# Attention and two feed-forward layers on one core: range checks after the attention, weights put together by shifts, a bias table per head, v in two float16 parts, a first pass of six 512-wide chunks

## The chip, the cores and the metric

The kernel runs on one core of a Trainium2 chip. The metric is the device time of one execution in microseconds (us); for the kernel before it is 632.22 us, the median of three runs (631.07 to 633.04). A core has five engines with a queue each: TensorE (PE in the profile; its weight loads are PEld), VectorE (DVE), ScalarE (ACT), GpSimd (POOL) and SyncE (SP, which issues the DMAs). Each works through its own instructions in the order of the program and waits on semaphores for the others.

## The reference

Attention over 2 x 8 heads of 768 rows of 64, in which a row sees the first `n_global` keys and its last `n_local` ones, with a bias per head; then two feed-forward layers over 1536 rows of 512.

```python
scores = scale * np.matmul(q, k.transpose(0, 1, 3, 2))
keep = is_global | is_local                       # 8 first keys, or 0 <= row - key < 96
dist = np.where(is_global & ~is_local, float(n_local), np.abs(rel))
bias = -slopes[:, None, None] * dist[None, :, :]  # slopes: 2 ** -(h + 1) for 8 heads
a = softmax(np.where(keep, scores + bias, -1e9))
x = np.matmul(a, v) as 1536 x 512
h = x @ w_in                                      # 512 x 2048
x = (h * np.clip(h + 3.0, 0.0, 6.0) / 6.0) @ w_out
h = np.maximum(x @ w_in2, 0.0)
return (h * h) @ w_out2
```

The feed-forward weights arrive as float64, that is as two 32-bit words a number.

## The kernel before, in words

**Attention.** The 1536 rows are 12 tiles of 128. For each tile PE transposes q and k (T, L413), multiplies them head pair by head pair (L479 in float32 for the first six tiles, which the code calls plain; L488 in split float32r for the last six), DVE adds the bias and finds the row's extreme in one instruction (L502), ACT takes the exponential and its sum (L515), the weights are transposed (by PE in the plain tiles, L554; by a DMA in the others, after a split into two float16 parts, L324 and L535), PE multiplies them by v (L603), DVE divides by the sum (L624 to L627), PE transposes the result (x_T, L647), and ACT and DVE write it as two float16 parts (x_hi, L324; x_lo, L656). Those parts, kept for all rows in three blocks of 512 columns (`xt`), are what the feed-forward layers read. In the last six tiles v is three bfloat16 parts (L324, L450), and the product takes five matmuls for each head and key block. q is first divided by the head's slope (L296), so that one bias table serves all heads.

**Weights.** A layer's 2048 inner columns are 16 chunks of 128; a chunk has two halves (of w_in and w_out), each a 128 x 512 tile of float64 pairs. For each of the 64 halves DVE masks the exponent (L777), ACT shifts it to float32's place (L781), DVE puts the sign to it (L784), takes the mantissa's upper bits (L790) and adds the lower word (L791), POOL multiplies the two (L796), and the result is written as two float16 parts (L324 or L326, then L804). A chunk takes one of 23 slots; 12 of these are there during the attention, the others take the attention's space when it has ended.

**Feed-forward.** An item is one chunk with one block of rows: 12 matmuls up (L848), a gate on ACT and DVE (L861 to L873), a split into two float16 parts (L324 or L326, L881), and 12 matmuls down (L914 in the first layer, L917 in the second), three for each product since both sides are in two parts. The first layer goes in three passes: in the first, 5 chunks with blocks of 256 rows, so that work for PE begins when two tiles of the attention are done; then 6 and 5 chunks with blocks of 512. The sums of a pass are added to `acc` in SBUF. The second layer is one pass of 16 chunks. In PSUM the attention holds 4 of 8 banks, the sums of the first pass 2 (`r_c`), the products up 2.

**Range checks.** Every split of a weight, and every tile of x, is squared and summed by ACT into a column of `gd` (L342); with the gates' sums these are compared at the end, and decide whether a slower version of the whole is to run afterwards.

**Order.** A planner (`Plan.order`) knows for each operation the engines that can do it, a duration, its buffers and a priority, and from these lays out once, when the program is built, what every engine does in which order; shifts of the priorities stand in a table (`SHIFT`). Where PE would wait early on, it puts in filler matmuls on a blank tile (L293).

Of the kernel before, what the change touches and what calls it, by code (L numbers as in the profile page):

```python
# [18 lines left out]
P = 128  # L19

N1 = 5
SLOTS_A = 12
SLOTS = 23
# [153 lines left out]
class Kern:  # L177
# [26 lines left out]
    def setup(self, pool):  # L204
# [48 lines left out]
        self.ebias_s = pool.tile([P, 1], F32, name="ebias_s")  # L253
        nc.gpsimd.memset(self.ebias_s, -(896.0 + 20.0 - EW) * 2.0 ** 23)
# [23 lines left out]
        self.scale_q("DVE", self.raw_t[0][0])  # L278
# [24 lines left out]
    def band_pools(self, ctx):  # L303
# [8 lines left out]
        self.kt = const.tile([P, 2, NP, 3, P], F32R, name="kt")  # L312
        pool = lambda name, bufs: ctx.enter_context(tc.tile_pool(name=name, bufs=bufs))
# [21 lines left out]
    def check_op(self, plan, view, deps, use, prio, n=512):  # L335
# [19 lines left out]
    def attention_ops(self, plan):  # L355
# [10 lines left out]
        for t in range(NT):  # L366
# [58 lines left out]
            for i, (c, t_, a_, b_, place) in enumerate(ends):  # L425
# [9 lines left out]
                if not plain:  # L435
                    qe.append(op(c + "_lo", {"DVE": 0.6}, lo, deps=[h_], use=[a_, b_], prio=vt - 4.3 + i / 10))
# [382 lines left out]
    def ffn_ops(self, plan, items, x_done):  # L819
# [9 lines left out]
        for it in items:  # L829
# [91 lines left out]
            for a in range(nacc):  # L921
# [7 lines left out]
                if acq:  # L929
                    state["g2"] = u  # L930
# [239 lines left out]
```

## Time and profile before

| | |
|---|---|
| median of three runs | 632.22 us |
| the profiled execution | 631.7 us |
| its span, first to last instruction | 629.9 us |
| PE busy | 599.6 us, 95% |
| DVE busy | 460.6 us, 73% |
| ACT busy | 331.8 us, 53% |
| POOL busy | 151.4 us, 24% |
| matmuls in the profile | 3887 |

Times in the views are microseconds from the span's start. The ends of matmuls are modelled, so what one costs in a dense stretch is read from the distance between two starts. A duration of DVE or ACT reaches a little into that of the next instruction.

### The profile page before, as it was taken

Reading aid. Unit: us, or ns where it says so; the run is one execution under the profiler, and the core shown is the slowest. Engines: PE = TensorE matmul, PEld = TensorE weight load, DVE = VectorE, ACT = ScalarE, POOL = GpSimd, SP = SyncE. Lnnn points to the kernel's source line nnn. Section 1 sums busy time; section 2 is a strip of 40 time slices with the busy share of each in tenths; the row PEclk is TensorE's granted clock in tenths of the full one; section 3 lists DMA queues with packets and bytes.
Section 4 is the critical chain, followed back from the end, with each engine's and each line's share of the span. In section 5 each row is a group of like instructions: output and inputs, shape, how many; then the busy total and the mean of one; then the engine's idle time right before and its main releaser. Section 6 shows DMA issues by size and latency. Waiting matters only on the chain.

```text
span 629.9 us, 10465 instructions
## 1 busy us (share of the span) xinstructions
PE 599.6 (95%) x3887; PEld 345.6 (55%) x3887; DVE 460.6 (73%) x1036; ACT 331.8 (53%) x778; POOL 151.4 (24%) x155
## 2 busy tenths in 40 slices
PE   7998798988989999999999999999999999999994
PEld 6887797777876544444444443444444444444442
DVE  4999989997889899999989999994333333333331
ACT  4997689888966665455586767552121111211111
POOL 1324427344442242314222431230000000000000
PEclk9999899999999999999999999999999999999998
DMA  9753648877652342324133232320010000100002
GB/s 181 192 139 107 181 107 187 149 133 109 124 126 93 101 134 100 101 67 135 67 101 101 67 132 69 101 67 1 1 67 1 0 1 0 68 1 0 1 0 72
DMA packets 84699, 53.32 MB, mean 85 GB/s; under 512 B 62368, under 2 KB 78752, under 8 KB 84640
## 3 DMA queue, kind: packets, MB, share of 16 engines
q1 hardware_dynamic: 84640, 52.57, 32.1%
q8 instruction: 32, 0.52, 0.3%
q14 instruction: 27, 0.22, 0.1%
HBM read 42.99 MB, written 3.15 MB: 73 GB/s over the span
## 4 chain that ended last, share of the span: by engine, by line
PE 46%; DVE 33%; DMA 10%; ACT 6%; issue 3%; POOL 0%; SPq 0%; DVEq 0%; ACTq 0%
PE bank L848 19%; PE bank L917 15%; DVE y L791 6%; DVE gt L881 5%; DMA wr<-in_moe_w_in_dram 4%; DVE e L784 4%; DMA pt<-ph 4%; DVE y L790 4%; PE bank L603 3%; PE bank L914 3%; DVE g L871 2%; DVE e L777 2%; DVE w L804 1%; DMA vp<-vp 1%; PE bank L479 1%
## 5 line engine op out<-in xcount | busy, mean ns | idle before, releaser
L848 PE MATMUL bank<-xt,w 128*128 128x512 f16 (+1 forms) x936 | 208.0, 338 | 1.1 <-DVE g L871 1.0
L796 POOL TENSOR_TENSOR y<-y,e 128x512 f32<-128x512 f32 x64 | 87.2, 1362 | 197.8 <-DVE y L791 91.5
L848 PEld LDWEIGHTS <-w 128*128 128x128 f16 x936 | 90.4, 98 | 72.1 <-issue 1.8
L914 PE MATMUL bank<-gt,w 128*128 128x256 f16 (+1 forms) x612 | 120.5, 317 | 0.9 <-DVE gt L881 0.8
L873 DVE SCALAR_TENSOR_TENSOR g<-bank,g 128x512 f32<-128x512 f32 x48 | 33.1, 690 | 117.3 <-ACT g L863 117.3
L863 ACT ACTIVATE g<-bank 128x512 f32<-128x512 f32 x48 | 28.5, 593 | 158.2 <-PE bank L848 158.0
L848 PE MATMUL bank<-xt,v 128*128 128x512 f16 x396 | 107.0, 379 | 0.0
L917 PEld LDWEIGHTS <-gt 128*128 128x128 f16 x576 | 56.3, 98 | 71.7 <-DVE gt L881 3.8
L917 PE MATMUL bank<-w,gt 128*128 128x512 f16 x324 | 86.8, 379 | 0.2 <-DVE gt L881 0.2
L881 DVE TENSOR_TENSOR gt<-g,gt 128x512 f16<-128x512 f32 (+1 forms) x99 | 73.9, 748 | 8.3 <-ACT gt L324 6.7
L914 PEld LDWEIGHTS <-w 128*128 128x128 f16 x612 | 59.4, 98 | 36.7 <-issue 1.7
L917 PE MATMUL bank<-v,gt 128*128 128x512 f16 x252 | 68.6, 379 | 1.2 <-DVE gt L881 1.2
L848 PEld LDWEIGHTS <-v 128*128 128x128 f16 x396 | 38.7, 98 | 46.3
L881 POOL TENSOR_TENSOR gt<-g,gt 128x256 f16<-128x256 f32 (+1 forms) x12 | 11.5, 959 | 201.8 <-DVE gt L326 192.7
L324 ACT ACTIVATE gt<-g 128x512 f16<-128x512 f32 (+1 forms) x64 | 34.5, 539 | 46.3 <-DVE g L871 37.1
L781 ACT ACTIVATE e<-e,ebias_s 128x512 int32<-128x512 int32 x64 | 45.7, 717 | 21.7 <-DVE e L777 21.3
L791 DVE SCALAR_TENSOR_TENSOR y<-wr,y 128x512 f32<-128x512 uint32 x64 | 51.8, 810 | 2.2
L784 DVE SCALAR_TENSOR_TENSOR e<-wr,e 128x512 int32<-128x512 int32 x64 | 47.5, 759 | 0.4 <-ACT e L781 0.4
L515 ACT ACTIVATE s<-s,mx 128x256 f32<-128x256 f32 (+1 forms) x96 | 46.0, 484 | 1.6 <-DVE mx L502 1.3
L861 ACT ACTIVATE g<-bank,half_s 128x512 f32<-128x512 f32 (+1 forms) x63 | 36.3, 577 | 19.7 <-PE bank L848 19.5
L914 PE MATMUL bank<-gt,v 128*128 128x512 f16 x144 | 38.9, 379 | 0.0
L871 DVE SCALAR_TENSOR_TENSOR g<-g,bank 128x512 f32<-128x512 f32 (+1 forms) x63 | 34.7, 552 | 4.9 <-ACT g L861 4.9
(118 smaller groups left out, 741.8 us busy)
## 6 DMA issues: line engine op xcount, KB each, us to landing
wr<-in_moe_w_in_dram SPq DMA_DIRECT2D x32, 512.0 KB, 4.0
wr<-in_moe_w_out_dram SPq DMA_DIRECT2D x32, 512.0 KB, 3.3
out_dram<-acc SPq DMA_DIRECT2D x12, 256.0 KB, 2.0
r<-in_q_dram SPq DMA_DIRECT2D x10, 256.0 KB, 3.4
r<-in_k_dram SPq DMA_DIRECT2D x10, 256.0 KB, 4.0
r<-in_v_dram SPq DMA_DIRECT2D x10, 256.0 KB, 3.6
acc<-in_q_dram SPq DMA_DIRECT2D x2, 256.0 KB, 4.6
acc<-in_k_dram SPq DMA_DIRECT2D x2, 256.0 KB, 5.1
```

The lines of the kernel that those rows point to most:

```text
L324: self.nc.scalar.activation(out=out, in_=in_, func=ACTF.Copy, scale=scale)
L515: nc.scalar.activation(out=s[:, e2, :n], in_=s[:, e2, :n], func=ACTF.Exp, scale=-1.0, bias=m["mx"][:, e2:e2 + 1], accum_out=sums[t][:, h:h ...
L781: nc.scalar.activation(out=d["e"], in_=d["e"], func=ACTF.Relu, scale=8.0, bias=self.eb)
L784: nc.vector.scalar_tensor_tensor(out=d["e"], in0=d["r"][:, :, 1], scalar=-2 ** 31, in1=d["e"], op0=ALU.bitwise_and, op1=ALU.bitwise_or)
L791: nc.vector.scalar_tensor_tensor(out=y.bitcast(F32), in0=d["r"].bitcast(U32)[:, :, 0], scalar=2.0 ** -32, in1=y, op0=ALU.mult, op1=ALU.add)
L796: self.tt(e)(out=y, in0=y, in1=d["e"].bitcast(F32), op=ALU.mult)
L848: nc.tensor.matmul(d["ps"], w[:, wi, 0, fs], xx[:, kd, o:o + n], start=(kd == 0 and i == 0), stop=(kd == self.KD - 1 and i == 2))
L861: nc.scalar.activation(out=g, in_=d["ps"], func=ACTF.Relu, scale=2.0 ** (EGD - EXW) / 6.0, bias=self.hf)
L871: nc.vector.scalar_tensor_tensor(out=g, in0=g, scalar=2.0 ** EGD, in1=ps, op0=ALU.min, op1=ALU.mult, **acc)
L881: self.tt(e)(out=gt[:, 1, :n], in0=d["g"], in1=self.val(gt[:, 0, :n]), op=ALU.subtract)
L914: nc.tensor.matmul(ps, w[:, wi, 1, s], g[:, gi, :n], start=st, stop=sp)
L917: nc.tensor.matmul(ps, g[:, gi, s], w[:, wi, 1, :], start=st, stop=sp)
```

## The change

- A bias table for each head (`first_h`, `band_h`, bfloat16) is made by 16 instructions on POOL at the start; q is no longer divided by the slope.
- A weight is put together from its two words by shifts: both words give a float32 pattern (two instructions on DVE), the sign and the upper exponent bits another (one), POOL multiplies them as before. ACT no longer takes part; it squares the second pattern as a range check instead.
- The checks on x and on the weights' split wait until the last tile of the attention is done; six more read v, which is loaded again for them.
- v is two float16 parts, and the product with v takes three matmuls in place of five.
- ACT makes the sum ready for the division (L620), in place of DVE.
- The first pass has 6 chunks with blocks of 512 rows. The splits of all six items of a block are kept (8 buffers in place of 3), and the products down go in two sweeps: first those of the output's columns 0 to 255, then those of 256 to 511, since two banks of PSUM hold only two of the four sums. 8 slots for chunks are there during the attention, 22 in all.
- The planner's durations, shifts and due times are other numbers.

```diff
-N1 = 5
-SLOTS_A = 12
-SLOTS = 23
+N1 = 6
+SLOTS_A = 8
+GB = N1 + 2
+SLOTS = 22
...
-    "v_0": 4.7, "v_1": 9.1, "v_2": -3.2, "v_3": -1.2, "v_glob": -5.2, "w_lo": 4.7, "w_load": -1.2, "w_man": 10.6,
+    "v_2": -3.2, "v_3": -1.2, "v_glob": -2.7, "v_load": -0.1, "w_exp": -23.4, "w_hi": 17.3, "w_lo": 1.3,
...
-    def scale_q(self, e, q):
-        self.tt(e)(out=q, in0=q, in1=self.qscale.unsqueeze(2).to_broadcast([P, self.H, self.D]), op=ALU.mult)
...
+        for to, src in ((self.first_h, self.first), (self.band_h, self.band.rearrange("p a c -> p (a c)"))):
+            for h in range(H):
+                nc.gpsimd.tensor_scalar(to[:, h], src, self.slope[h] * float(D) ** 0.5, 1.0, op0=ALU.mult, op1=ALU.mult)
...
-        self.sums2.append(plan.op("chk", {"ACT": 0.72}, emit, deps=deps, use=use, prio=prio))
+        self.sums2.append(plan.op("chk", {"ACT": 0.82}, emit, deps=deps + self.late, use=use, prio=prio))
...
-                vp_t[t] = self.vp_p.tile([P, 3, H * D], BF16, tag="vp", name="vp")
+                vp_t[t] = self.vp_p.tile([P, 2, H * D], F16, tag="vp", name="vp")
...
+                nc.vector.scalar_tensor_tensor(out=vp_t[t][:, 1], in0=raw[2].rearrange("p h d -> p (h d)"), scalar=2.0 ** EX,
+                                               in1=vp_t[t][:, 0], op0=ALU.mult, op1=ALU.subtract)
...
-                            out=s[:, e2, :n], in0=m["q"]["ps"][e2][:, p % 2, :n], in1=bias, scale=-self.slope[2 * p + e2],
+                            out=s[:, e2, :n], in0=m["q"]["ps"][e2][:, p % 2, :n], in1=bias, scale=-1.0 / float(D) ** 0.5,
...
-                                for l, parts in ((0, 3), (1, 2)):
+                                for l, parts in ((0, 2), (1, 1)):
...
-                nc.vector.tensor_scalar(rs, sums[t], 1e-9, 2.0 ** -EX, op0=ALU.add, op1=ALU.mult)
+                    nc.scalar.activation(out=rs, in_=sums[t], func=ACTF.Copy, scale=sx, bias=1e-9 * sx)
...
+                    nc.vector.tensor_scalar(y, d["r"][:, :, 1], 3, 0x7FFFFFFF, op0=ALU.logical_shift_left, op1=ALU.bitwise_and)
...
+                    nc.vector.scalar_tensor_tensor(out=y, in0=d["r"][:, :, 0], scalar=29, in1=y,
+                                                   op0=ALU.logical_shift_right, op1=ALU.bitwise_or)
...
+                    nc.vector.tensor_scalar(s, d["r"][:, :, 1], -2 ** 28, 0x30000000 ^ ((EW - 1) << 23), op0=ALU.bitwise_and,
+                                            op1=ALU.bitwise_xor)
...
+                    nc.scalar.activation(out=junk, in_=d["e"].bitcast(F32), func=ACTF.Square, scale=2.0 ** (128 - EW),
+                                         accum_out=self.gd3[:, i:i + 1])
...
-        r_h, r_c, r_g, r_t = self.r_h, self.r_c, Ring(3), Ring(2)
+        r_h, r_g, r_t = self.r_h, Ring(GB if self.fast else 3), Ring(2)
...
+            self.down_ops(plan, it, (0, 1) if half else (0, 1, 2, 3), vt + PELAG, state, acc_ops, x2_ops)
+            if half:
+                block.append(it)
+                if it["last"]:
+                    for k, i2 in enumerate(block):
+                        self.down_ops(plan, i2, (2, 3), vt + PELAG + 1 + 0.2 * k, state, acc_ops, x2_ops)
...
-            passes = [[(N1, 256), ((17 - N1) // 2, 512), ((16 - N1) // 2, 512)], [(16, 512)]]
+            passes = [[(N1, 512), ((17 - N1) // 2, 512), ((16 - N1) // 2, 512)], [(16, 512)]]
```

On PE, before, ahead of the fourth tile's x_T (L647), feed-forward matmuls (L848, L914) already stand between those of the attention:

```order
L848 LDWEIGHTS w_172
L848 MATMUL bank<-xt_0_165,w_172 128x256
L914 LDWEIGHTS w_171
L914 MATMUL bank<-gt,w_171 128x256
L479 MATMUL bank<-k_plain,q_plain 128x128 x8
L554 MATMUL bank<-ident,s 128x128 x4
L647 MATMUL bank<-ident,x 128x128 x4
```

The same place now, with x_T on L653, the product with v on L595 and the filler on L290:

```order
L595 MATMUL bank<-r_412,pt 128x64
L546 MATMUL bank<-ident,s 128x128 x8
L595 MATMUL bank<-r_933,pt 128x64
L653 MATMUL bank<-ident,x 128x128 x4
L479 MATMUL bank<-kt,qz_199 128x128 x4
L546 MATMUL bank<-ident,s 128x128 x4
L290 LDWEIGHTS blank
L290 MATMUL bank<-blank 128x256
```

Up to the fourth x_T there is now no feed-forward matmul, while 68 of the 79 fillers stand there; the first one comes after the fourth tile's x parts.

On POOL, behind the branch into the kernel, the tables now stand first, ahead of the copies of the global keys (L568; L576 before). Before:

```order
L576 COPY kg_plain<-k_plain 128x64 x2
L576 COPY k_plain<-kg_plain 128x2x32 x2
L796 TENSOR_TENSOR y<-y,e 128x512
L576 COPY k_plain<-kg_plain 128x2x32
L296 TENSOR_TENSOR r_511<-r_511,qscale 128x512
```

Now:

```order
L312 TENSOR_SCALAR first_h<-first 128x128 x8
L312 TENSOR_SCALAR band_h<-band 128x384 x8
L568 COPY kg_plain<-k_plain 128x64 x2
L568 COPY k_plain<-kg_plain 128x2x32 x4
L802 TENSOR_TENSOR y<-y,e 128x512 x2
```

The division of q (L296) is gone, and 16 instructions have come in front of the first copies.

## Rows read from the trace of the kernel before

**Rows 1.** The page's first part: busy time, share and instructions of each engine.

```profile
PE 599.6 (95%) x3887; PEld 345.6 (55%) x3887; DVE 460.6 (73%) x1036; ACT 331.8 (53%) x778; POOL 151.4 (24%) x155
```

**Rows 2.** Windows by stage: from:to length, busy (count) per engine, clock, DMA, GB/s.

```profile
6.00:183.00 177.00, 159.56 (x1791) 140.32 (x1792) 157.64 (x458) 148.59 (x423) 71.37 (x73) 0.98 0.69 148
...
200.00:340.00 140.00, 139.87 (x661) 64.45 (x660) 131.66 (x237) 85.51 (x168) 43.11 (x33) 1.00 0.31 102
...
430.00:622.00 192.00, 191.55 (x889) 86.73 (x887) 68.44 (x151) 27.81 (x47) 1.16 (x1) 1.00 0.03 12
```

**Rows 3.** Timeline of PE, 6 to 21 us: start, length, engine, line, shape, count.

```profile
7.09 0.63 PE L413 MATMUL bank<-ident,acc 128*128 128x128 f32 x4 [1.83 <-DVE acc L296]
...
16.96 0.56 PE L603 MATMUL bank<-acc,pt 128*128 128x64 f32 x4
17.36 0.49 PE L293 MATMUL bank<-blank 128*128 128x256 bf16 x3
17.78 1.16 PE L479 MATMUL bank<-k_plain,q_plain 64*128 64x128 f32 x16
18.87 1.09 PE L554 MATMUL bank<-ident,s 128*128 128x128 f32 x8
19.80 0.60 PE L647 MATMUL bank<-ident,x 128*128 128x128 f32 x4
```

**Rows 4.** Timeline of PE, 114 to 117.5 us.

```profile
114.84 0.76 PE L603 MATMUL bank<-vp,pt 128*128 128x64 bf16 x20 [0.78 <-DMA pt<-ph]
115.53 0.98 PE L488 MATMUL bank<-kt,qz 64*128 64x256 f32 x12
116.44 0.76 PE L603 MATMUL bank<-vp,pt 128*128 128x64 bf16 x20
```

**Rows 5.** Timeline of PE, 178 to 184 us: the last tile's x_T.

```profile
179.26 0.49 PE L848 MATMUL bank<-xt,w 128*128 128x256 f16 x3
179.59 0.49 PE L914 MATMUL bank<-gt,w 128*128 128x256 f16 x3
...
181.55 0.60 PE L647 MATMUL bank<-ident,x 128*128 128x128 f32 x4
```

**Rows 6.** Timeline of PE, 55 to 57.5 us: the fourth tile's x_T.

```profile
55.49 0.60 PE L647 MATMUL bank<-ident,x 128*128 128x128 f32 x4
```

**Rows 7.** Groups by line: busy us, mean ns of one, idle before them.

```profile
L791 DVE SCALAR_TENSOR_TENSOR y<-wr,y 128x512 f32<-128x512 uint32 x64 | 51.8, 810 | 2.2
L784 DVE SCALAR_TENSOR_TENSOR e<-wr,e 128x512 int32<-128x512 int32 x64 | 47.5, 759 | 0.4 <-ACT e L781 0.4
L781 ACT ACTIVATE e<-e,ebias_s 128x512 int32<-128x512 int32 x64 | 45.7, 717 | 21.7 <-DVE e L777 21.3 <-DVE k_plain L576 0.2
L790 DVE TENSOR_SCALAR y<-wr 128x512 int32<-128x512 int32 x64 | 36.7, 573 | 0.0
L777 DVE TENSOR_SCALAR e<-wr 128x512 int32<-128x512 int32 x64 | 28.7, 454 | 1.9 <-DMA wr<-in_moe_w_in_dram 1.7
L624 DVE TENSOR_SCALAR rs<-sum 128x8 f32<-128x8 f32 x12 | 6.3, 523 | 0.0
```

**Rows 8.** Window of the attention, the checks of L342 alone: ACT's busy time (count).

```profile
6.00:183.00 177.00, 20.74 (x58) 0.98 0.69 148
```

**Rows 9.** Timeline of PE, 66 to 82 us: the longest wait.

```profile
73.33 2.39 PE L479 MATMUL bank<-k_plain,q_plain 64*128 64x128 f32 x16 [3.40 <-DVE mx L502]
```

**Rows 10.** Windows of 2 us around it; PEclk 1.00 is 2.4 GHz.

```profile
74.00:76.00 2.00, 2.00 (x17) 1.78 (x16) 1.97 (x6) 1.69 (x6) 0.22 (x1) 0.50 0.60 199
...
80.00:82.00 2.00, 2.00 (x21) 1.92 (x21) 1.97 (x5) 1.46 (x6) 0.00 (x0) 1.00 0.00 0
```

**Rows 11.** Lines L576, L535 and L502: smallest, median, largest ns, or groups by shape.

```profile
L576 POOL CAST kg<-kt x1: 287/287/287, 86.8 to 86.8; 128x128 fp32r<-128x128 f32 x1
...
L535 POOL TENSOR_TENSOR ph<-s,ph 128x256 f16<-128x256 f32 x4 | 2.7, 675 | 4.6 <-ACT ph L324 4.6
...
L502 DVE CUSTOM_DVE_ANT_0 s<-bank,band x80: 406/418/426, 16.1 to 165.3; 128x256 f32<-128x256 f32 x80
```

More of the change, by code (lines that the diff above doesn't have):

```diff
@@ L620, in attention_ops, with total @@
             xx = {}
+            sx = 2.0 ** -EX if plain else 1.0
+            def total(e, t=t, xx=xx, sx=sx):
+                xx["rs"] = rs = self.sm_p.tile([P, H], F32, tag="rs", name="rs")
+                if e == "ACT":
+                    nc.scalar.activation(out=rs, in_=sums[t], func=ACTF.Copy, scale=sx, bias=1e-9 * sx)
+                else:
+                    nc.vector.tensor_scalar(rs, sums[t], 1e-9, sx, op0=ALU.add, op1=ALU.mult)
             def norm(e, t=t, xx=xx):
-                rs = self.sm_p.tile([P, H], F32, tag="rs", name="rs")
-                nc.vector.tensor_scalar(rs, sums[t], 1e-9, 2.0 ** -EX, op0=ALU.add, op1=ALU.mult)
+                rs = xx["rs"]
                 nc.vector.reciprocal(rs, rs)
@@ new lines, in weight_ops, with load_v @@
+                o7 = op("w_hi", {"ACT": 0.62, "VEC": 0.42}, hi, deps=[o6], use=[b_y], acq=[b_w], prio=vt)
+                o8 = op("w_lo", {"VEC": 0.69, "POOL": 1.2}, lo, deps=[o7], use=[b_y, b_w], prio=vt)
+                ch["ready"].append([o7, o8])
+        for t in range(self.TPB, self.NTILE) if self.fast else ():
+            b_wr, d = r_wr.new(), {}
+            def load_v(e, t=t, d=d):
+                r = self.wr_p.tile([P, self.DM, 2], I32, tag="wr", name="wr")
+                d["r"] = r.bitcast(F32).rearrange("p f t -> p (f t)")[:, :self.DM]
+                nc.sync.dma_start(out=d["r"].rearrange("p (h d) -> p h d", d=self.D), in_=self.rows(self.v, t))
+            o1 = op("v_load", {"SP": 0.45}, load_v, acq=[b_wr], prio=vt + 20, wire=1.46)
+            self.check_op(plan, lambda d=d: d["r"], [o1], [b_wr], vt + 30, 2.0 ** EX)
@@ L919, in ffn_ops @@
[L919 to L932 removed]
+            it["g"] = lambda d=d: d["gt"]
@@ L935, in ffn_ops, with down_ops, g2 @@
             self.guard_ops(plan, gates)
+    def down_ops(self, plan, it, outs, prio, state, acc_ops, x2_ops):
+        nc = self.nc
+        l, n, ch, vt = it["l"], it["n"], it["chunk"], it["vt"]
+        if it["first"]:
+            state["bufs"] = {a: self.sums_bank(it["early"]) for a in outs}
+            state["tiles"] = {}
+        bufs, tiles = state["bufs"], state["tiles"]
+        def g2(e, a):
+            if it["first"]:
+                tiles[a] = self.bank(bufs[a].tag)
+            w, g = ch["w"], it["g"]()
+            s = slice(a * P, (a + 1) * P)
+            for i in range(3):
+                st, sp = it["first"] and i == 0, it["last"] and i == 2
+                if l == 0:
+                    wi, gi = ((0, 0), (0, 1), (1, 0))[i]
+                    nc.tensor.matmul(tiles[a], w[:, wi, 1, s], g[:, gi, :n], start=st, stop=sp)
+                else:
+                    wi, gi = ((0, 0), (1, 0), (0, 1))[i]
+                    nc.tensor.matmul(tiles[a], g[:, gi, s], w[:, wi, 1, :], start=st, stop=sp)
+        it.setdefault("g2", {})
+        for a in outs:
+            b_c = bufs[a]
+            acq = [b_c] if it["first"] else []
+            order = [state.get("g2")] if it["first"] else [it["prev2"]["g2"][a]]
+            u = plan.op("down", {"PE": 0.648}, lambda e, a=a: g2(e, a), deps=order + it["got"],
+                        use=[ch["buf"], it["b_g"]] + ([] if acq else [b_c]), acq=acq, prio=prio + a * 0.01)
+            it["g2"][a] = u
+            if acq:
+                state["g2"] = u
+            if it["last"]:
+                self.acc_ops(plan, it, a, tiles, b_c, u, acc_ops, x2_ops, vt)
```

235 lines of the change are left out of this document (102 added, 133 removed).

## The prediction, made before the changed kernel ran

> **What bounds the kernel now.** First the page's busy shares, then the windows by stage, then PE's timeline for what one matmul costs and for the landmarks between stages. PE is busy for 95% of the span [rows 1], so PE's work is the floor; the windows show where it isn't met. From 430 to 622 us 889 matmuls of 512 columns start in 192 us, 0.216 us each, and nothing stands between them [rows 2]. The same holds from 200 us on: 661 in 140 us are 0.212, a few 256-wide ones among them [rows 2]. So from about 200 us the time is a count of matmuls. During the attention, from 6 to 183 us, no engine is full: PE is busy for 159.6 us of 177, DVE for 157.6, ACT for 148.6 [rows 2]. PE's figure flatters, since it holds modelled ends and 34 fillers, so I count its work by steps between starts. A float32 product with v takes 0.40 us for its 4 records, that is two matmuls, 0.20 each; 8 score matmuls (16 records) 1.09 us, 0.136 each; 8 transpositions 0.93 us, 0.116 each [rows 3]; 20 matmuls of 64 columns 0.69 us, 0.0345 each; 12 split score matmuls 0.91 us, 0.076 each [rows 4]; a 256-wide feed-forward matmul 0.33/3 = 0.11 us [rows 5].
>
> With the order's counts the attention on PE is 232 x 0.116 + 88 x 0.136 + 88 x 0.20 + 144 x 0.076 + 440 x 0.0345 = 82.6 us, and 582 matmuls of 256 columns stand ahead of the last x_T, 64.0 us: 146.6 us of work between 7.1 us, where PE's first transposition starts [rows 3], and 181.55 us, the last x_T [rows 5]. That is 84% of 174.5 us; 28 us are lost. DVE, at 89% of the window, sets the pace there: PE's longest wait is for it, 3.40 us for L502 [rows 9]. Behind the last x_T, which takes 0.4 us, stand 138 matmuls of 256 columns and 1944 of 512: 15.2 + 419.9 = 435.1 us, so PE could end at 617; it ends at 622 [rows 2], 5 us lost. The profiled execution is 631.7 us, 9.4 us more than PE's last matmul at 622.3 (the last sums, the copies out and 1.8 us outside the span), and 0.5 us under the median of the runs; I add that 0.5 at the end.
>
> **The change part by part.**
>
> *v in two parts.* 440 matmuls become 264, 176 x 0.0345 = 6.1 us less for PE [rows 4]. On DVE, ACT and POOL four instructions a tile become two.
>
> *512 columns in the first pass.* 720 matmuls at 0.11 = 79.2 us become 360 at 0.216 = 77.8, but a sixth chunk moves into this pass (432 instead of 360), out of a later one. Over the kernel PE gains 1.4 us. More matters when they can run: the order has no feed-forward matmul ahead of the fourth x_T, where the kernel before has 36 of them; it has 276 of 512 columns (59.6 us) ahead of the last one, and 2028 behind it, 438.0 us.
>
> *Weights by shifts.* A half costs DVE 0.454 + 0.759 + 0.573 + 0.810 = 2.60 us before [rows 7]. Now it is two TENSOR_SCALAR and one two-input instruction. The new forms aren't in the trace; the nearest rows are L777 and L790 (0.454 and 0.573) and L784 and L791 (0.759 and 0.810), so a half costs between 1.67 and 1.96 us. I take 1.84. ACT's L781 at 0.717 us is replaced by a check of about the same length (L342: 20.74 us for 29 pairs, 0.715) [rows 7, 8], so ACT gains nothing, but DVE no longer waits behind ACT in the middle of a half. By the order 18 to 20 halves stand ahead of the last tile before and 17 now: 49.0 us become 31.3, 17.7 less.
>
> *Other work of DVE there.* The sum's preparation goes to ACT, 12 x 0.523 = 6.3 us [rows 7]; six divisions of q, about 4 us; 25 gates of 256 columns become 12 of 512, with their splits about 8 us less; splits of weights about 6 less. The split of v, more copies of p on DVE and one more transposed copy add about 7. With the weights 35 us in all: 157.6 becomes about 123.
>
> *Checks after the attention.* They take ACT 20.74 us of the window [rows 8]. With fewer casts of v and of p it goes from 148.6 to about 115. The 94 checks come back behind the attention, 94 x 0.715 = 67 us over some 270 us in which the weights are still being made; ACT was busy for 85.5 of 140 us there [rows 2]. Cover: 54 us of idle ACT in each 140. Should they hold up a weight's split in ACT's queue, one costs 0.7 us, and only if PE has no item left.
>
> *Tables on POOL.* 16 instructions ahead of POOL's other work. The trace has no such instruction; the nearest are a 128-wide cast of 0.287 us and a 256-wide two-input one of 0.675 [rows 11]. From the first, 8 x 0.29 + 8 x 0.6 = 7 us; from the second, 8 x 0.34 + 8 x 1.0 = 11. They begin when DVE has the base tables, shortly before the first L502, and the second tile's L502 begins at 16.1 [rows 11] and needs one table at a time: hidden, or up to 3 us late. On the other side the division of q in front of the first transposition goes, for which PE waited 1.83 us [rows 3]; q itself must still land. I take 0 for both, with -1 to +3. L502 ran beside POOL all through the attention and took 406 to 426 ns in all 80 cases [rows 11], so I let POOL cost it nothing. The Trainium skill (SBUF — State Buffer, "SBUF: two separate sides") says that POOL and a DVE instruction with two SBUF inputs shut each other out for a whole instruction; L502 reads one input from PSUM, so by the rule too the price is 0, and it would be up to 8 x 0.6 us if the rule took in every DVE instruction.
>
> **The sum.** Up to the fourth x_T everything is attention of the first six tiles. The order puts about as much DVE work there as before (48.4 us against 49.0, by steps), and PE has 164 x 0.116 + 88 x 0.136 + 72 x 0.20 = 45.4 us, so I let this stretch end at 60 us, a little later than the 55.5 us of before [rows 6], since nearly all of the first six tiles is now in it. From there to the last x_T PE has 76.5 + 59.6 - 45.4 = 90.7 us, DVE about 75 and ACT about 68. PE is now the longest. Taken at 92 to 93% of full, better than the 84% of before as DVE has room, it is 98 us. Then 0.4 + 438.0 us, 4 us lost (5 before) and 9.4 at the end: 60 + 98 + 0.4 + 438.0 + 4 + 9.4 = 609.8, with the 0.5 about **610 us**, 22 us or 3.5% less. Of that 7.5 us are PE's work and 14.5 us its idle time.
>
> **The rivals.**
>
> *Chains, not DVE, set the pace.* An attention tile is a chain from PE over DVE, ACT, POOL and a DMA back to PE (PE waits 0.78 us for the DMA transposition in one place [rows 4]), with three buffers a step. If PE stays at 84% for the whole attention, 136.1 us take 162: the last x_T is at 169, the total 621. With weights late after the end (8 slots ready in place of 12) up to 626. For it: L502's wait of rows 9; against it: DVE at 89% explains that wait.
>
> *PE nearly gapless.* At 97% from the fourth x_T at 57 us: 93.5 us, total 602; with the lower prices of the new DVE forms and a stretch of 50 us at the start 596.
>
> *Slower.* PE's clock. After the wait of 3.40 us PE was granted half its clock: at 74 to 76 us it stood at 0.50, that is 1.2 GHz, and at 80 us at 2.4 again [rows 9, 10]; the some 6.7 us from the wait's end cost about 3.3 us more than at full clock. The stretch up to the fourth x_T now has no feed-forward matmuls to bridge waits, only 68 fillers. If it ran at 1.2 GHz throughout, its 45.4 us would take 45.4 more, less some 8 us of idle time: 647. The change is slower once over 30 us of that work run at 1.2 GHz. The Trainium skill (TensorE: Matmul & The Clock Gate, "HAM oscillation — how this bites in real kernels") warns of just this, a matmul loop that waits between bursts and starts every burst at half clock. The trace speaks against it here: from 6 to 183 us the mean clock is 0.98 [rows 2], fillers and all.
>
> *Nothing.* The time saved in the attention is given back after it, since PE is full from 200 us on and DVE is at 94% from 200 to 340 us [rows 2]. But DVE's weights shrink there too (some 45 halves, 0.76 us less each), so a return of all 22 us is hard to see.
>
> **How the numbers follow.** Forecast (602 to 617) 0.50; chains (617 to 628) 0.24; gapless (590 to 602) 0.18; slower by the clock 0.05; nothing 0.03. The range leaves out about 0.1 on each side: 598 to 623. A measurement of this kernel tells 0.3%, 2 us, from no change: faster 0.92, same 0.02, slower 0.06.
>
> **What would show it.** The fourth x_T near 60 us and the last near 158 (if it is past 168, the chains are right; before 152, PE is gapless); PE's first feed-forward matmul behind 55 us; L502 at 418 ns as before; the new weight forms at 0.45 to 0.57 and 0.75 to 0.81 us; DVE under 85% in the attention; the clock at 1.00 in every window up to 60 us; from there on 0.216 us a matmul without gaps over 1 us. The forecast is wrong in its reason if DVE is still the engine that PE waits for, or if the gain comes from behind the attention.

## The result and the profile after

| | before | after | forecast |
|---|---|---|---|
| median, us | 632.63 (631.07 to 633.49) | 607.58 (606.88 to 609.21) | 610 (598 to 623) |
| profiled execution, us | 631.7 | 607.48 | 609.8 |
| fourth x_T starts | 55.5 | 63.4 | 60 |
| last x_T starts | 181.6 | 159.4 | 158 |
| PE's last matmul ends | 622.3 | 598.2 | |
| lost behind the last x_T | 5.2 | 0.3 | 4 |

Four runs each. The changed kernel takes 0.961 of the time before, 95% interval 0.9583 to 0.9638: 25 us less. "Lost" is here and below the time from the last x_T to PE's end, less 0.4 for x_T itself and less the feed-forward matmuls behind it at 0.11 us (256 columns) and 0.216 us (512).

The page's first part, after, and the shares by engine of the chain that ended last:

```profile
PE 591.9 (98%) x3396; PEld 307.8 (51%) x3396; DVE 393.5 (65%) x906; ACT 330.5 (55%) x827; POOL 150.4 (25%) x156
...
PE 83%; DMA 6%; DVE 6%; issue 2%; ACT 1%; SPq 0%; POOL 0%; DVEq 0%; POOLq 0%
```

The same chain before:

```profile
PE 46%; DVE 33%; DMA 10%; ACT 6%; issue 3%; POOL 0%; SPq 0%; DVEq 0%; ACTq 0%
```

Beside [rows 1]: DVE is busy for 67 us less, ACT for about as long as before, PE for 98% of the span. DVE held a third of the chain that ended last and now holds 6%. Windows by stage, after (from:to length, busy and count of PE, PEld, DVE, ACT and POOL, clock, DMA share, GB/s):

```profile
6.00:160.00 154.00, 149.53 (x1348) 106.64 (x1349) 126.39 (x377) 116.51 (x344) 61.66 (x77) 1.00 0.71 158
...
200.00:340.00 140.00, 140.00 (x650) 63.52 (x649) 116.07 (x216) 95.15 (x217) 47.30 (x35) 1.00 0.33 106
...
406.00:598.00 192.00, 192.00 (x892) 86.89 (x890) 71.64 (x155) 36.33 (x70) 4.67 (x4) 1.00 0.08 23
```

Against [rows 2] the attention takes 154 us in place of 177, and DVE is busy for 82% of it (126.4 of 154) where it was 89%. In the last 192 us PE starts 892 matmuls where it started 889: a 512-wide matmul costs what it did, 0.215 us. The clock is 1.00 in all three. PE's timeline, after, at its start, at the fourth x_T and at the last (start, length, engine, line, shape, count, idle time before):

```profile
6.68 0.63 PE L410 MATMUL bank<-ident,acc 128*128 128x128 f32 x4 [1.18 <-DVE band L281]
...
63.43 0.61 PE L653 MATMUL bank<-ident,x 128*128 128x128 f32 x4
...
65.28 1.04 PE L290 MATMUL bank<-blank 128*128 128x256 bf16 x8
...
66.59 1.67 PE L897 MATMUL bank<-xt,w 128*128 128x512 f16 x7
...
159.43 0.60 PE L653 MATMUL bank<-ident,x 128*128 128x128 f32 x4
159.87 2.75 PE L973 MATMUL bank<-gt,w 128*128 128x512 f16 x12
```

The first feed-forward matmul starts at 66.6 us, and the last x_T at 159.4 where [rows 5] have 181.55. What PE waits for in the whole kernel, after (waiting line, what it waited for: total us, times, longest):

```profile
PE bank L595 <- DMA r<-in_v_dram: 1.4, 1, 1.4
PE bank L410 <- DVE band L281: 1.2, 1, 1.2
...
PE bank L595 <- DMA pt<-ph: 1.0, 2, 0.8
```

The 3.40 us that PE once waited for DVE's extremes [rows 9] have no counterpart: the longest wait inside the attention is 1.4 us, for v from memory. Apart from the start (the band table and the blank tile, 2.3 us) PE waits for DVE only 1.3 us in all, where L502 alone took 4.9 before, and most of the gain lies ahead of the last x_T. So neither of the signs came by which the forecast would have been wrong in its reason. The 68 fillers up to the fourth x_T do hide some waits there (a_nofill, below).

**Where the 24.2 us between the profiled executions came from.** The last x_T is 22.1 us earlier. Of these 10.5 are PE's counted work ahead of it: 146.6 us before; now 82.6 - 6.1 + 276 x 0.216 = 136.1. Another 11.3 are PE's idle time there (28 of 174.5 us before, 16.6 of 152.7 now), and 0.4 the earlier start. Some 3 of the 11.3 us are PE's lower clock around 74 us before [rows 10], not waiting. Behind the last x_T the count is 2.9 us longer, the loss 4.9 shorter, and the end 0.1 shorter: 22.1 - 2.9 + 4.9 + 0.1 = 24.2. PE's work is 7.6 of it, its idle time 16.6.

### The profile page after: what moved, and what is told of

Same layout as the page of the kernel before. It is cut to its first block, busy times and chain, and to the rows that moved or that the text cites. A ratio compares the mean times of both kernels' runs of the same rounds, so it can differ in the third digit from the quotient of the medians.

```text
span 605.7 us, 9487 instructions
## 1 busy us (share of the span) xinstructions
PE 591.9 (98%) x3396; PEld 307.8 (51%) x3396; DVE 393.5 (65%) x906; ACT 330.5 (55%) x827; POOL 150.4 (25%) x156
## 4 chain that ended last, share of the span: by engine, by line
PE 83%; DMA 6%; DVE 6%; issue 2%; ACT 1%; SPq 0%; POOL 0%; DVEq 0%; POOLq 0%
PE bank L897 38%; PE bank L976 21%; PE bank L973 17%; PE bank L595 2%; DMA wr<-in_moe_w_in_dram 2%; DMA wr<-in_moe_w_out_dram 2%; DMA pt<-ph 1%; PE bank L470 1%; PE bank L546 1%; DVE s L494 1%; DVE y L820 1%; PE bank L410 1%; PE bank L479 1%; DVE ph L527 1%; PE bank L290 1%
## 5 line engine op out<-in xcount | busy, mean ns | idle before, releaser
L897 PE MATMUL bank<-xt,v 128*128 128x512 f16 x576 | 155.4, 379 | 0.0
L897 PE MATMUL bank<-xt,w 128*128 128x512 f16 x576 | 149.3, 379 | 0.3 <-DVE g L920 0.3
L802 POOL TENSOR_TENSOR y<-y,e 128x512 f32<-128x512 f32 x64 | 89.6, 1405 | 171.5 <-DVE y L820 146.8
L897 PEld LDWEIGHTS <-v 128*128 128x128 f16 x576 | 56.4, 98 | 67.9
L897 PEld LDWEIGHTS <-w 128*128 128x128 f16 x576 | 55.0, 98 | 63.6 <-issue 0.5
L973 PE MATMUL bank<-gt,v 128*128 128x512 f16 x288 | 77.9, 379 | 0.0
L973 PE MATMUL bank<-gt,w 128*128 128x512 f16 x288 | 72.5, 379 | 0.4 <-DVE w L810 0.4
L930 DVE TENSOR_TENSOR gt<-g,gt 128x512 f16<-128x512 f32 x84 | 64.8, 772 | 4.7 <-ACT gt L324 3.4
L930 POOL TENSOR_TENSOR gt<-g,gt 128x512 f16<-128x512 f32 x12 | 14.9, 1246 | 185.7 <-DVE gt L326 179.3
L820 DVE SCALAR_TENSOR_TENSOR y<-wr,y 128x512 int32<-128x512 int32 x64 | 51.1, 810 | 0.0
L910 ACT ACTIVATE g<-bank,half_s 128x512 f32<-128x512 f32 x48 | 32.8, 683 | 32.2 <-PE bank L897 32.0
L831 ACT ACTIVATE junk<-e 128x512 bf16<-128x512 f32 x64 | 40.0, 625 | 16.9 <-DVE e L826 16.2
L973 PEld LDWEIGHTS <-v 128*128 128x128 f16 x288 | 28.2, 98 | 34.0
L973 PEld LDWEIGHTS <-w 128*128 128x128 f16 x288 | 27.6, 98 | 32.3 <-DVE w L810 0.9
L826 DVE TENSOR_SCALAR e<-wr 128x512 int32<-128x512 int32 x64 | 31.1, 492 | 16.1 <-DMA wr<-in_moe_w_in_dram 8.4
```

The costliest lines, as they stand in the source:

```text
L802: self.tt(e)(out=y, in0=y, in1=d["e"].bitcast(F32), op=ALU.mult)
L820: nc.vector.scalar_tensor_tensor(out=y, in0=d["r"][:, :, 0], scalar=29, in1=y, op0=ALU.logical_shift_right, op1=ALU.bitwise_or)
L826: nc.vector.tensor_scalar(s, d["r"][:, :, 1], -2 ** 28, 0x30000000 ^ ((EW - 1) << 23), op0=ALU.bitwise_and, op1=ALU.bitwise_xor)
L831: nc.scalar.activation(out=junk, in_=d["e"].bitcast(F32), func=ACTF.Square, scale=2.0 ** (128 - EW), accum_out=self.gd3[:, i:i + 1])
L897: nc.tensor.matmul(d["ps"], w[:, wi, 0, fs], xx[:, kd, o:o + n], start=(kd == 0 and i == 0), stop=(kd == self.KD - 1 and i == 2))
L910: nc.scalar.activation(out=g, in_=d["ps"], func=ACTF.Relu, scale=2.0 ** (EGD - EXW) / 6.0, bias=self.hf)
```

## The experiments

The theory of the prediction, in short DVE: DVE sets the pace of the attention, the change takes work off it, and what is left is PE's count. Its rivals: ACT (the checks that were put off are what matters), PE's smaller count alone, and the order: the planner lays all engines out anew for every set of numbers, and this layout is a good one. All versions but a_nofill and the `f_` ones are planned anew, so that their times hold both the edit and another order. In the `f_` ones the order of the changed kernel is kept, instruction by instruction, with the added ones in between; in a_nofill it is kept without the fillers. "Against after" is the difference of the two ratios to the kernel before, times 632 us. The landmarks are those of one profiled execution each.

| version | median, us | ratio to before, 95% | against after | fourth x_T | last x_T | lost behind |
|---|---|---|---|---|---|---|
| after | 607.58 | 0.961 (0.9583 to 0.9638) | | 63.4 | 159.4 | 0.3 |
| b_shift | 621.11 | 0.983 (0.9798 to 0.9862) | | 55.4 | 175.1 | 2.0 |
| b_v2 | 631.57 | 0.997 (0.9946 to 0.9995) | | 57.6 | 175.1 | 12.8 |
| a_oldw | 645.69 | 1.0208 (1.0169 to 1.0246) | +38 | 60.9 | 173.5 | 18.3 |
| a_chk_early | 620.87 | 0.9824 (0.979 to 0.9858) | +13.5 | 60.3 | 169.8 | 0.1 |
| a_v3 | 623.95 | 0.9893 (0.9856 to 0.9931) | +18 | 63.4 | 170.1 | 2.2 |
| a_scale | 622.09 | 0.9849 (0.9824 to 0.9874) | +15 | 57.1 | 175.3 | 2.1 |
| a_oldtab | 622.11 | 0.9854 (0.9817 to 0.9891) | +15 | 52.2 | 167.4 | 9.2 |
| a_nofill | 610.87 | 0.9676 (0.9632 to 0.972) | +4 | 65.2 | 163.0 | 0.5 |
| jit | 614.9 | 0.9728 (0.9712 to 0.9744) | +7.5 | 64.0 | 168.7 | 1.3 |
| f_dve | 629.4 | 0.9961 (0.9938 to 0.9985) | +22 | 67.3 | 166.9 | 12.2 |
| f_act | 612.94 | 0.9706 (0.969 to 0.9723) | +6 | 65.1 | 162.1 | 1.8 |
| f_pe | 611.25 | 0.9666 (0.9645 to 0.9686) | +3.5 | 64.7 | 164.6 | 1.2 |

PE's mean granted clock goes with the times: over the runs it is 0.997 after, 0.998 in f_act and f_pe, 0.994 in jit, 0.991 in a_nofill, 0.988 in f_dve, 0.985 in a_oldtab and 0.980 in a_oldw. So a price below can hold both what PE waits for and the clock that it is granted less behind waits. An estimate from these figures, the difference in clock times the length: up to 4 us in a_nofill, 6 in f_dve, 7 in a_oldtab and 11 in a_oldw.

**One part alone: b_shift, b_v2.** The kernel before with the weights by shifts, and with v in two parts.

```diff
# b_shift
+                    o2 = op("w_exp", {"VEC": 0.34}, shift, deps=[o1], use=[b_wr], acq=[b_y], prio=vt)
+                    o3 = op("w_man", {"VEC": 0.6}, last3, deps=[o2], use=[b_wr, b_y], prio=vt)
+                    o4 = op("w_sign", {"VEC": 0.34}, sign_s, deps=[o1], use=[b_wr], acq=[b_e], prio=vt)
# b_v2
-                                for l, parts in ((0, 3), (1, 2)):
+                                for l, parts in ((0, 2), (1, 1)):
```

> The kernel before with one part alone: weights by shifts, with the check of the sign pattern on ACT. DVE saves some 17 us of 158 in the attention and more behind it, ACT nothing. Theory DVE: 619 to 626 us. Theory ACT: 629 to 633 us. Theory order: 629 to 633 us.

> The kernel before with one part alone: v in two float16 parts. PE saves 6.1 us in the attention, DVE, ACT and POOL together 24 instructions. If DVE sets the pace there (theory DVE), PE's saving counts little and what DVE saves counts: 627 to 632 us. If PE's work counts in full: 624 to 627 us.

The shifts alone take 10.7 us off (0.983), inside what DVE expected: 6.4 at the last x_T, 3.3 behind it. v in two parts alone brings 1.9 us (0.997): the last x_T is as early as with the shifts, but 12.8 us are lost behind it where 5.2 were. PE's longest waits behind the last x_T, of b_v2:

```profile
PE bank L908 <- DVE gt L875: 2.9, 4, 1.9
PE bank L908 <- POOL gt L875: 2.0, 1, 2.0
```

These are the splits of the gates; DVE, which still makes the weights the old way, is busy for 134.0 of the 140 us from 200 to 340. So a microsecond won in the attention lasts only if DVE also keeps up behind it; the "nothing" rival describes this version, not the change.

**The weights the old way in the changed kernel: a_oldw.**

```diff
-                    o2 = op("w_exp", {"VEC": 0.42}, shift, deps=[o1], use=[b_wr], acq=[b_y], prio=vt)
...
-                    self.upper.append(op("w_pow", {"ACT": 0.82}, upper, deps=[o4], use=[b_e], prio=vt))
...
-                    nc.scalar.activation(out=d["e"], in_=d["e"], func=ACTF.Relu, scale=8.0, bias=self.ebias)
+                    nc.scalar.activation(out=d["e"], in_=d["e"], func=ACTF.Relu, scale=8.0, bias=self.eb)
```

> The changed kernel with one part undone: each weight is put together as before (mask, ACT's exponent step, sign, two mantissa steps), and the range check of the sign pattern is left out. DVE gets about 0.8 us more for each of 17 halves ahead of the last tile, some 13 us, so 137 us of 153. Theory DVE (the gain comes from DVE's relief, weights first): 616 to 622 us, the last x_T near 170 us, DVE near 90% in the attention. Theory ACT (the gain comes from the checks that left ACT): 607 to 611 us. Theory order (the planner's new numbers make the gain, whatever the work is): 607 to 611 us.

It is slower than the kernel before, and past what all three theories expected. The last x_T comes 14 us later and 18 us are lost behind it. Window from 400 to 450 us, and PE's waits, of a_oldw:

```profile
400.00:450.00 50.00, 41.61 (x171) 16.70 (x169) 43.16 (x73) 26.80 (x55) 16.37 (x12) 0.93 0.37 116
```

```profile
PE bank L889 <- ACT w L326: 4.1, 3, 2.7
PE bank L889 <- ACT v L326: 3.2, 2, 2.0
```

PE starts 171 matmuls in 50 us where 232 would fit (50 / 0.216): it waits for the splits of weights that are still being made. These are weights of the second layer: the first layer's last product starts at 373.8 us, 200.2 us after the last x_T, against 197.5 in the changed kernel with 15 matmuls (3.2 us) fewer to do, so nothing more is lost up to there. The direction is DVE's; the size, far over what DVE expected, is not.

**Other parts undone, planned anew: a_chk_early, a_v3, a_scale, a_oldtab.** The checks not put off; v in three bfloat16 parts again; the division of q and one bias table again; the planner's old shifts, preferences and due times. One or two lines of each edit:

```diff
# a_chk_early
-        self.sums2.append(plan.op("chk", {"ACT": 0.82}, emit, deps=deps + self.late, use=use, prio=prio))
+        self.sums2.append(plan.op("chk", {"ACT": 0.82}, emit, deps=deps, use=use, prio=prio))
# a_v3
-                                for l, parts in ((0, 2), (1, 1)):
+                                for l, parts in ((0, 3), (1, 2)):
# a_scale
+            sq = lq if t == 0 else op("scale", {"VEC": 0.69, "POOL": 1.2}, lambda e, raw=raw: self.scale_q(e, raw[0]), deps=[lq], use=[bq],
+                                      prio=vt - 8)
# a_oldtab
-ATT0 = 13.12
-ATT = 7.66
+ATT0 = 6.2
+ATT = 10.26
```

> The changed kernel with one part undone: the range checks on x and on the weights' split no longer wait for the last tile, and get due times as before. ACT gets some 27 checks of 0.715 us, 19 us, into the attention: from about 115 to 134 us of 153. Theory DVE: 607 to 612 us, since ACT has room. Theory ACT: 616 to 624 us. Theory order: 607 to 612 us.

> The changed kernel with one part undone: v in three bfloat16 parts and five matmuls for each product with v. PE gets 176 matmuls of 0.0345 us back, 6.1 us, and DVE, ACT and POOL two instructions a tile more. If PE is the longest engine of the attention now, all of it shows: 613 to 617 us. If idle time takes it up: 607 to 610 us.

> The changed kernel with one part undone: one bias table for all heads and q divided by the head's slope; the 16 instructions on POOL are gone, 12 divisions on DVE or POOL are back. DVE gets up to 12 x 0.7 us: 8 us of 153. Theory DVE with PE now the longest: 607 to 613 us. If the tables on POOL cost something at the start, it is 605 to 607 us.

> The changed kernel with all its parts, but with the planner's shifts, preferences and due times of before. Theory DVE: the work is the same, so most of the gain stays: 610 to 618 us. Theory order: the gain is gone, 625 to 635 us. Theory ACT: 610 to 618 us.

Each costs 13 to 18 us; with a_oldw's 38 the five make 100 us, four times what the whole change gained. So they can't be prices of parts that add up. a_scale shows it best. Its window of the attention:

```profile
6.00:160.00 154.00, 139.94 (x1245) 101.35 (x1246) 120.90 (x358) 111.36 (x327) 65.55 (x72) 0.98 0.68 149
```

DVE is busy for 120.9 us, less than the 126.4 of the changed kernel, and PE still starts 103 matmuls fewer in the stretch (fillers among them): neither DVE nor ACT nor PE became fuller, so it isn't their load. Whether it is the layout alone, or the division that again stands in front of a tile's transposition, wasn't told apart. By DVE's load a_chk_early, a_v3 and a_scale should have come out close to the changed kernel; all three are far slower. a_chk_early, taken alone, falls where ACT expected it (616 to 624); f_act below, with as many checks at the kept order, doesn't bear that out.

a_oldtab speaks for the order: it has all the work of the change and keeps only 9 of the 25 us, less than DVE expected and more than the order theory did. Less work without numbers that fit it isn't enough. In a_chk_early PE waits 6.2 us for the transposition by DMA, 1.0 after.

```profile
PE bank L595 <- DMA pt<-ph: 6.2, 2, 3.2
```

**The order alone: jit.** One due time of the planner, by 0.3%; the work is the same.

```diff
-ATT = 7.66
+ATT = 7.68
```

> The changed kernel with all its work, and one of the planner's numbers moved by 0.3%: the due time between two tiles of the attention, 7.68 for 7.66. The planner lays out another order on every engine. Theory fit: 612 to 624 us. Theory that a part's own work makes its price: 606 to 610 us.

7.5 us slower, as the theory of the fit expected, with the last x_T 9.3 us later and the same work. Its window and PE's longest sum of waits:

```profile
6.00:160.00 154.00, 144.87 (x1294) 103.26 (x1295) 123.64 (x372) 117.30 (x347) 66.67 (x81) 0.99 0.72 160
```

```profile
PE bank L595 <- DMA pt<-ph: 5.3, 4, 3.9
```

A new plan can thus cost 7.5 us by itself, and a part undone with a new plan can't be read as the price of the part. Hence the next three.

**Prices at a fixed order: f_dve, f_act, f_pe.** Twice the two-input instruction of a weight (64 more on DVE); 28 more checks on ACT, beside the tiles of x and the first weights; 176 more 64-column matmuls in the last six tiles, as many as v in two parts took away.

```diff
# f_dve
-                    nc.vector.scalar_tensor_tensor(out=y, in0=d["r"][:, :, 0], scalar=29, in1=y,
-                                                   op0=ALU.logical_shift_right, op1=ALU.bitwise_or)
+                    for _ in range(2):
+                        nc.vector.scalar_tensor_tensor(out=y, in0=d["r"][:, :, 0], scalar=29, in1=y,
+                                                       op0=ALU.logical_shift_right, op1=ALU.bitwise_or)
# f_act
+        self.nc.scalar.activation(out=junk, in_=src, func=ACTF.Square, scale=2.0 ** -9, accum_out=self.spare)
# f_pe
+                        for a, b in (mm[:2 * len(sl_)] if t >= TPB else []):
+                            nc.tensor.matmul(ps[:, h], a, b, start=True, stop=True)
```

> The changed kernel in its own order on every engine, with one DVE instruction more for each of the 64 halves: the one that brings in the lower word is issued twice (the second changes nothing). DVE gets 64 x 0.74 us, 12.6 us of them ahead of the last tile, what the old way of putting weights together took more. Theory DVE's work (DVE's load is what the parts' own prices are made of): 617 to 625 us. Theory fit (a part undone is dear since the planner lays out another order for it, not by its own work): 608 to 613 us.

> The changed kernel in its own order, with a check more on ACT right behind each x_hi and behind each split of the first eight chunks: 28 x 0.715 us, 20 us, nearly all ahead of the last tile. The checks after the attention stay. Theory ACT's work: 618 to 624 us, as with the checks moved forward (620.87). Theory fit: 608 to 613 us.

> The changed kernel in its own order, with 176 matmuls of 64 columns more in the products with v (the first two terms of each group are computed once more, ahead of the group that counts): PE gets the 6.1 us of v in three parts. Theory PE's work (PE is the longest engine of the attention): 612 to 615 us, as much as the work. Theory that the three parts cost 16 us by themselves: 620 us or more.

Windows of f_dve, and PE's waits in it:

```profile
6.00:160.00 154.00, 145.22 (x1313) 104.55 (x1314) 133.62 (x383) 115.53 (x341) 61.86 (x76) 1.00 0.69 153
...
200.00:340.00 140.00, 133.78 (x610) 59.79 (x608) 130.02 (x224) 87.08 (x200) 49.47 (x37) 0.99 0.32 100
```

```profile
PE bank L898 <- DVE g L921: 6.0, 5, 2.2
PE bank L595 <- DMA pt<-ph: 5.8, 3, 2.7
```

The line of the doubled instruction in f_dve (busy us, mean ns), beside 51.1 us for 64 of them in the changed kernel:

```profile
L821 DVE SCALAR_TENSOR_TENSOR y<-wr,y 128x512 int32<-128x512 int32 x128 | 108.9, 856 | 2.2
```

So 57.8 us more on DVE cost 22 us, more than was expected; in the profiled execution 19, 7.4 of them at the last x_T and 11.8 behind it, where DVE is at 93% from 200 to 340 us (130.02 of 140) and PE waits 6.0 us for the gates (L921). These 57.8 us are a little more than the 54 us by which the weights became cheaper, 64 x (2.60 - 1.76), the latter by the rows further down: put back at the same order, they take nearly the whole gain. Two things make this price high rather than low: the order was laid out without this work, and the ten runs spread from 625.15 us at a mean clock of 0.997 to 633.07 at 0.984, so the clock has a share. At the clock of the changed kernel it is some 16 to 18 us. a_oldw's DVE is busy for 449.6 us over the whole kernel and f_dve's for 447.8, nearly the same load, and a_oldw is 16 us slower: that rest is not the size of DVE's load. Window of f_act:

```profile
6.00:160.00 154.00, 147.23 (x1334) 105.03 (x1335) 125.59 (x373) 133.17 (x396) 61.33 (x77) 1.00 0.73 157
```

ACT goes from 116.5 to 133.2 us there and the time grows by 6, not by the 10 to 16 that the theory of ACT's work expected: ACT has room, but not all of it for nothing. 176 matmuls on PE, 6.1 us by [rows 4], cost 3.5 us, a little under what was expected: PE's idle time takes up a part. In the profiled execution the last x_T is 5.2 us later, but the fourth, ahead of all added matmuls, already 1.3: so much a landmark moves from one execution to another. Against the changed kernel, then, DVE's work for the weights is worth some 16 to 22 us, the checks of this stretch about 6, v's matmuls about 4. That is the order of size of 25, and with b_shift's 10.7 us, where the weights alone are changed and planned anew, the direct support for DVE.

**The fillers and the clock: a_nofill.** No filler matmuls.

```diff
-FILL = 0.6
+FILL = 0.0
```

> The changed kernel without the 79 filler matmuls of the first tiles (the 20 at the very start stay). If the fillers hold the clock up in the stretch without feed-forward matmuls: a granted clock of 0.5 for a part of the first 63 us and 612 to 640 us. If the attention's own matmuls are enough: 606 to 609 us and the clock at 1.00.

4 us slower, between the two expectations. Windows of 2 us of a_nofill; from 38 to 42 us the clock is lower:

```profile
30.00:32.00 2.00, 0.43 (x4) 0.43 (x4) 2.00 (x5) 1.71 (x6) 0.18 (x1) 1.00 1.02 218
...
36.00:38.00 2.00, 1.24 (x12) 1.10 (x10) 1.63 (x7) 1.93 (x8) 0.00 (x0) 1.00 0.35 78
38.00:40.00 2.00, 1.88 (x10) 1.58 (x10) 1.26 (x5) 0.83 (x2) 0.59 (x1) 0.55 0.13 33
40.00:42.00 2.00, 2.00 (x18) 1.88 (x18) 1.38 (x3) 1.34 (x5) 0.69 (x2) 0.59 0.63 194
42.00:44.00 2.00, 1.79 (x16) 1.56 (x15) 2.00 (x10) 0.61 (x2) 1.33 (x2) 1.00 0.20 68
```

PE waited 1.85 us ahead of 31.57 and 0.88 ahead of 38.12; from 38 to 42 it was granted 0.55 and 0.59, mostly the lower level (1.2 GHz), and then the full clock again. 4 us at 0.57 lose about 1.7 us, and the fourth x_T comes 1.8 us later. That is the profiled execution, 610.10 us at a mean clock of 0.994. The other three runs took 608.64 us at 0.996, 611.64 at 0.989 and 614.22 at 0.986: the time goes with the clock, and by the four means the clock accounts for nearly all of the 4 us. So its price is real and small; the rival that let the whole stretch fall to half did not occur even without fillers. Without them the waits of this stretch show too: up to 65 us PE waits once each for a DMA (1.8 us), for DVE's band table (1.8) and for DVE's L494 (1.5), besides shorter waits.

## Why the prediction was right

The time came 2.4 us under the forecast, for the reason given, with three terms off by two to four microseconds that partly cancel: that it came this close is in part luck. The forecast also had no term for how well the order is laid out, and one due time moved by 0.3% gives 614.9 us.

**DVE's load.** Predicted about 123 us in the attention, measured 126.4; ACT about 115, measured 116.5. A half's three instructions, grouped by line after (busy us, mean ns of one):

```profile
L820 DVE SCALAR_TENSOR_TENSOR y<-wr,y 128x512 int32<-128x512 int32 x64 | 51.1, 810 | 0.0
L826 DVE TENSOR_SCALAR e<-wr 128x512 int32<-128x512 int32 x64 | 31.1, 492 | 16.1 <-DMA wr<-in_moe_w_in_dram 8.4 <-DMA wr<-in_moe_w_out_dram 7.7
L816 DVE TENSOR_SCALAR y<-wr 128x512 int32<-128x512 int32 x64 | 28.9, 462 | 2.5 <-DMA wr<-in_moe_w_in_dram 2.0 <-POOL w L810 0.3 <-DMA wr<-in_moe_w_out_dram 0.2
```

0.810 + 0.492 + 0.462 = 1.76 us, where 1.84 was taken between bounds of 1.67 and 1.96: the forms of [rows 7] with the same shape were good neighbours. In the median they are the same, 0.42 us for one input and 0.68 to 0.69 for two, before and after; what differs between the means is time in which DVE was held up beside POOL (last section). f_dve shows that this load counts most of the three that were added, b_shift that it pays by itself.

**The stretch to the fourth x_T: mis-sized.** 60 predicted, 63.4 measured. PE needs 45.4 us of work there and has 56.7 (from 6.7), 80%; DVE (41.7 of 54) and ACT (43.9) are not full either:

```profile
6.00:60.00 54.00, 52.80 (x520) 47.55 (x521) 41.69 (x152) 43.90 (x144) 21.01 (x36) 1.00 0.78 182
```

PE's 97.8% here holds fillers and modelled ends. No engine is full by its work, so here the chain from engine to engine, the "chains" rival, most likely sets the pace; the spread of PE's waits in a_nofill over DVE, ACT and DMAs fits that, but no run shows it. A margin over the 55.5 us of before was no working; the 84% of before, put to the counts, would have given 61 (7 + 45.4 / 0.84).

**From there to the last x_T: mis-sized the other way.** 90.7 us of work took 96.0, 94.5% where 92 to 93% was taken and the "gapless" rival had 97. The "chains" rival (84% for the whole attention, last x_T at 169) is refuted for this order: over the whole attention it is 136.1 of 152.7, 89%. It is about what jit, a_chk_early and a_v3 show, with their last x_T at 168.7 to 170.1: the rival was a fair description of the attention under another order, and the forecast did not say how much its 92% hung on the one that was laid out.

**Behind the last x_T: mis-sized.** 4 us lost predicted, 0.3 measured; PE's waits from 160 to 600 us come to 0.3 us. The cheaper weights alone bring the loss from 5.2 to 2.0 us (b_shift); the prediction had seen the cause (some 45 halves, 0.76 us less each) and did not put it into the sum.

**Sum.** 63.4 + 96.0 + 0.4 + 438.0 + 0.3 + 9.3 = 607.4, against 60 + 98 + 0.4 + 438.0 + 4 + 9.4. The counts held to the last figure; +3.4, -2.0 and -3.7 are the errors, beside 0.1 at the end.

**Checks.** Predicted: out of the attention, about 67 us behind it, hidden there. L342 alone, after:

```profile
6.00:160.00 154.00, 0.00 (x0) 1.00 0.71 158
160.00:400.00 240.00, 59.48 (x166) 1.00 0.31 100
```

ACT goes from 85.5 to 95.2 us in 200 to 340, and PE loses nothing there. Hidden, as said.

**Tables.** 8 x 0.300 + 8 x 0.513 = 6.5 us on POOL, just under the lower bound of 7. L312, then L494 (L502 before), after (smallest, median, largest ns), and the first use of a wide table on DVE's timeline:

```profile
L312 POOL TENSOR_SCALAR first_h<-first x8: 298/300/300, 7.3 to 9.5; 128x128 bf16<-128x128 f32 x8
L312 POOL TENSOR_SCALAR band_h<-band x8: 512/513/516, 9.8 to 13.5; 128x384 bf16<-128x384 f32 x8
```

```profile
L494 DVE CUSTOM_DVE_ANT_0 s<-bank,band_h x80: 408/419/427, 14.4 to 144.6; 128x256 f32<-128x256 f32 x80
```

```profile
14.37 0.42 DVE L494 CUSTOM_DVE_ANT_0 s<-bank,band_h 128x256 f32<-128x256 f32 x1 [1.02 <-POOL kg_plain L568]
```

They were not quite hidden: the last table ends at 14.0 us, the copies of the global keys (L568) stand behind the tables on POOL, and DVE waits 1.02 us for POOL ahead of the second tile's first L494. PE shows 0.2 us for it. That lies within the -1 to +3 that was allowed. The gain in front of the first transposition is 0.4 us (7.09 to 6.68), because PE now waits for the band table's own work (L281), which had stood behind the division.

**POOL beside L494.** 408, 419 and 427 ns, as before (406, 418, 426 in [rows 11]), with POOL busy for 61.7 of the 154 us around it: a price of 0, as the rows of before said. The Trainium skill (SBUF — State Buffer, "SBUF: two separate sides") lets POOL hold up a DVE instruction if that one runs in a 2-port mode or has two SBUF inputs; L494 has one input from PSUM, and the trace agrees. What POOL did hold up are the weights' own instructions (last section); the price taken for them held that already, being made of means.

**Clock.** 1.00 in every window up to 60 us; the slower rival did not occur. The Trainium skill's warning (TensorE: Matmul & The Clock Gate, "HAM oscillation — how this bites in real kernels") is borne out on a small scale by a_nofill, 0.55 at 38 us.

**What stays open.** How much of the 25 us the layout holds. Fixed-order prices say that DVE's weights carry most of it; jit says that a plan for the same work can lie 7.5 us off, a_oldtab 15. The 512-wide blocks of the first pass, the fewer slots and the sum's preparation on ACT were not undone one by one, and the bias tables only under a new plan. Whether a still better one exists wasn't searched for; no version here beats the changed kernel. Nor was it told apart why PE waits longer for the DMA transposition in the worse plans (5.1, 6.2 and 5.3 us in a_oldw, a_chk_early and jit). The transposition itself is about as quick there, 3.5, 2.8 and 3.1 us in the median from issue to landing against 2.9, and f_dve, at the kept order, waits 5.8 us with 2.8: so it is rather what goes before it that is late.

## What to carry to other kernels

Count the bottleneck engine's work stage by stage from distances between starts, then ask of each stage who keeps it from being met: here the count gave 574 of 607 us exactly, and only the idle shares had to be judged. A saving on one engine in an early stage lasts only if the engines that the later stage needs keep up too (b_v2 kept 1.9 us of 6.4). In a kernel whose order a planner lays out, price a part at a fixed order, by adding its work back: undone and planned anew, five parts seemed to be worth 100 us of a gain of 25.

## What the runs showed of the hardware that was not expected

- The two-input int32 instruction (L820) takes 684 ns in the median and 1757 at most; its mean of 810 is set by 11 of the 64. All 11 began while POOL was in the middle of an instruction (L802, L810 or L930), and each ended 0.546 to 0.551 us behind the end of that one; none of the other 53 (673 to 704 ns) began so. So DVE was held up there until POOL was done, 8.1 us in all. Of the one-input L816 and L826, 12 of 128 were long (over 480 ns), each ending 0.28 us behind the end of a POOL instruction. The 64 of L820 (smallest, median, largest ns), and one of the 11 with the POOL instruction that it waited for (start, length):

```profile
L820 DVE SCALAR_TENSOR_TENSOR y<-wr,y x64: 673/684/1757, 25.6 to 412.7; 128x512 int32<-128x512 int32 x64
```

```profile
230.54 1.58 POOL L802 TENSOR_TENSOR y<-y,e 128x512 f32<-128x512 f32 x1 [5.49 <-DVE y L820]
230.91 1.76 DVE L820 SCALAR_TENSOR_TENSOR y<-wr,y 128x512 int32<-128x512 int32 x1
```

- A 384-wide TENSOR_SCALAR from float32 to bfloat16 on POOL takes 0.513 us, a 128-wide one 0.300: from one to the other 0.83 ns a column, which leaves about 0.19 us for the rest of an instruction (an estimate from these two widths).
- A sum of squares on ACT with its accumulator read takes two records, 0.625 and 0.188 us; the sum's preparation (L620) 0.200 us on ACT where DVE took 0.523 [rows 7].
- Added one at a time at the kept order, 57.8 us on DVE cost 22 us, 28 checks on ACT (18.0 us of its busy time) 6 and 6.1 us on PE 3.5: none of them is free, and none costs all of itself.
